# One reciprocal for the forward scans' first values, and a reordered start, in a gated-linear-attention and SoLU kernel

## The chip, the cores and the metric

The kernel runs on one core of one Trainium2 chip, as one launch. The metric is the device time of that launch in microseconds (us); "before" is the kernel without the change. In the profile PE is TensorE's matmuls, PEld its weight loads, DVE is VectorE, ACT ScalarE, POOL GpSimd and SP SyncE, which only issues DMAs. L12 is line 12 of the kernel before.

## The reference, cut to what matters

```python
# q, k, v, alpha: (4, 8, 768, 48); alpha lies between 0.8 and 1.0
for t in range(768):
    state = alpha[:, :, t, :, None] * state + k_t (outer) v_t      # per batch and head
    y[:, :, t] = q_t @ state
x = y as (3072 tokens, 384)
h = x @ w_in                                    # 384 -> 1024
solu = h * softmax(h)
ln = (solu - mean) / sqrt(var + 1e-6) * g_ln
out = ln @ w_out                                # 1024 -> 384
```

All is float32, except that the three weights arrive as float64.

## The kernel before, in words

**Tiling.** The 768 tokens are cut into G = 6 groups of 128. A group holds those 128 tokens of all four batches, thus 512 columns. Inside a group the recurrence is done in one piece: with the products of alpha along the tokens, the scores of the group's tokens are a masked matrix, and what came before enters through a state per head, updated once a group.

**Layout of the attention.** Alpha, k and q are turned so that channels lie on partitions and tokens along the row: 12 rows of 129 values (`aT`, `hT`, `kT`, `qv` and `qe`), in three parts of four rows (NP = 4). Parts 0 and 1 hold the first 32 channels of the eight heads, part 2 the last 16 of all heads. In group 0 TensorE turns them (`turned`, L158, against the identity `ident`), with the last 16 channels copied together first by ScalarE (`ends_of`, L151); later groups use VectorE's transposes (`firsts`, `lasts`, `alpha_T`).

**The scans.** `scan_back` (L206) forms with a VectorE scan the product of alpha from the end of the group backwards; its first column (`h4[:, :, 1]`) is the decay over the whole group, and the keys are multiplied by it. `scan_on` (L211) forms the same products forwards, as a scan that starts from the reciprocal of that column, with `seed` as its second operand: all zero except for the first value of each row. For each part it limits the column from below to 1e-13 (`least`, L218), takes the reciprocal into one of two seed tiles (L219) and scans in place in `aT` (L220, recorded as L204). In its call for part 2 it also copies the column to `fend` (L215), which a check at the end of the kernel compares with 1e-13 (L949). The queries are multiplied by the result. Where any of the checks fails, a general path runs after this one.

**The start (group 0, L643 to L760).** SyncE's queue loads alpha, k, q, v and the first raw weights, in this order, from L643 on; ScalarE's queue loads the identity, the mask, `parity` and the gains (L644 to L648). VectorE sets `ones`, `mone` (minus one, a bias of the alpha check) and others; GpSimd zeroes `vn`, `unit`, `seed`, `state` and `kg`. `warm(18)` (L673, products in L446) multiplies ones by ones on TensorE until alpha is there. Then alpha is turned into three PSUM tiles, ScalarE copies them (L677) and VectorE scans back; k is turned; then scan on for part 2, the keys' products (L685), scan on for part 0, the queries' products for parts 2 and 0 (L693), scan on for part 1 and its product. ScalarE's `apart` (L246) splits part 2 of the queries by parity. `scores` (L274) multiplies queries and keys, first half (heads 0 to 3), then second half; `masked` (L288) multiplies by the mask on VectorE; `read_values` (L352) multiplies the values by the masked scores. After that VectorE turns the float64 weights into float32 in eight pieces (`bits`, L584), between the steps of the first group's up-projection (`up_mm`, `up_act`), and ScalarE checks their range (`in_range`, L574).

**Order.** Every engine runs its instructions in the order written in the code. Group 1's attention is written out at L744 to L800, between the down-projections of group 0 (`down`, `finish`); group 2's scans, keys and first forward scans at L801 to L811. Then a hand-written plan (`usual` and `first`, L815 to L826) places the steps of the next group's attention among the eight up-projections of the present group; "on2 on0 on1" are the three forward scans, which for groups 3 to 5 come with the second up-projection.

**Around the change.** `finish` (L506) takes four small VectorE steps (L519 to L528), GpSimd's power (L532) and ScalarE's scaling, then issues the output. `up_act` (L396) frees the PSUM tile of an up-projection with L405. `decay` (L258) multiplies the state by the group's decay on GpSimd, which `ends_of_decay` (L242) and the DMAs of `move_lasts` and `move_firsts` (L230 to L240) bring into place, and `read_state` (L344) multiplies the queries by it. `keys` (L226) multiplies keys by the backward products on GpSimd, and `queries` (L253) the queries by the forward ones. `alpha_over` (L192) checks on ScalarE that alpha lies within -1 and 1. `far` keeps sums of the weights' check.

Of the kernel before, what the change touches and what calls it, by code (L numbers as in the profile page):

```python
# [9 lines left out]
FP = mybir.dt.float32  # L10
# [3 lines left out]
AF = mybir.ActivationFunctionType  # L14
ALU = mybir.AluOpType
AX = mybir.AxisListType
P = 128
# [15 lines left out]
def fast_path(ctx, tc, q, k, v, alpha, moe_w_in, moe_w_out, moe_g_ln, out):  # L33
# [12 lines left out]
    nc = tc.nc  # L46
# [5 lines left out]
    NP = H // 2  # L52
    NB = H + NP
# [5 lines left out]
    LEAST = 1e-13  # L59
# [5 lines left out]
    const = pool("const", 1)  # L65
    ring = pool("ring", 3)
    work = pool("work", 2)
    small = pool("small", 4)
# [4 lines left out]
    ps_a = pool("ps_a", 1, space=PS)  # L73
# [13 lines left out]
    mone = const.tile([P, 1], FP, name="mone")  # L87
# [8 lines left out]
    fend = const.tile([P, G, NB], FP, name="fend")  # L96
# [12 lines left out]
    SW = P + 1  # L109
# [1 line left out]
    lots = [lot[:, 768 * i : 768 * i + 768] for i in range(4)]  # L111
    q64 = lot[:, 0 : 2 * H * SW].rearrange("p (c h t) -> p c h t", c=2, h=H)
    aT = const.tile([P, NB, SW], FP, name="aT")
    seed = [const.tile([P, NP, SW], FP, name=f"seed{i}") for i in range(2)]
    unit = const.tile([P, NP, SW], FP, name="unit")
    hT = const.tile([P, NB * SW + 2], FP, name="hT")
    h4 = hT[:, 0 : NB * SW].rearrange("p (j s) -> p j s", s=SW)
# [25 lines left out]
    def load_first(src, dst, g):  # L143
        t = slice(g * P, (g + 1) * P)
        for b in range(0, B, 2):
            nc.sync.dma_start(
                out=by_token(dst)[:, b : b + 2].rearrange("p b h d -> p (b h) d"),
                in_=src[b : b + 2, :, t].rearrange("b h p d -> p (b h) d"),
            )
# [42 lines left out]
    def alpha_over(g):  # L192
        x = an.rearrange("p h u d -> p (h u d)")
        sq = one.tile([P, 768], FP, name="sq").bitcast(U8)[:, 0 : x.shape[1]]
        for i, sign in enumerate((1.0, -1.0)):
            nc.scalar.activation(  # L196
                out=sq, in_=x, func=AF.Relu, scale=sign, bias=mone, accum_out=over[:, g, i : i + 1]
            )

    def scan(out, data, start, flip):  # L200
        a, o, s = (x.rearrange("p j s -> p (j s)") for x in (data, out, start))
        if flip:
            a, o, s = a[:, ::-1], o[:, ::-1], s[:, ::-1]
        nc.vector.tensor_tensor_scan(out=o, data0=a, data1=s, initial=1.0, op0=ALU.mult, op1=ALU.add)  # L204

    def scan_back(g, i):  # L206

        part = slice(NP * i, NP * i + NP)
        scan(h4[:, part], aT[:, part], unit, True)

    def scan_on(g, i):  # L211
        part = slice(NP * i, NP * i + NP)
        s = seed[i % 2]
        if i == 2:
            nc.vector.tensor_copy(out=fend[:, g], in_=h4[:, :, 1])  # L215

        least = small.tile([P, NP, 1], FP, name="least")
        nc.vector.tensor_scalar(out=least, in0=h4[:, part, 1:2], scalar1=LEAST, scalar2=None, op0=ALU.max)  # L218
        nc.vector.reciprocal(out=s[:, :, 0:1], in_=least)  # L219
        scan(aT[:, part], aT[:, part], s, False)  # L220

    def keys_T(g):
        firsts(kn, kT[:, 0:H])
        lasts(kn, kT[:, H:NB])
# [21 lines left out]
    def apart():  # L246
        for i in range(2):
            nc.scalar.mul(
                out=qv[:, H : 2 * H, 0:P].rearrange("p (j i) t -> p j i t", i=2)[:, :, i], in_=qe[:, :, 0:P],
                mul=parity[:, i : i + 1],  # L250
            )
# [22 lines left out]
    def scores(g, half, a=None):  # L274
        a = a or banks("a", [NP, P])
        for i in range(NP):
            h = half * NP + i
            for kb, qb in ((h, h), (H + h // 2, H + h)):
                for b in range(B):
                    nc.tensor.matmul(  # L280
                        a[b][:, i], lhsT=kT[quarter(b), kb], rhs=qv[quarter(b), qb, 0:P], start=kb == h, stop=kb != h,
                        tile_position=(32 * b, 0), skip_group_check=True,
                    )
        masks[half] = a
# [158 lines left out]
    def warm(n, ps=ps_o, tag="o"):  # L443
        t = ps.tile([P, 512], FP, tag=tag, name="warm")
        for i in range(n):
            nc.tensor.matmul(t[:, 0:P], lhsT=ones, rhs=ones, start=True, stop=True)  # L446
# [124 lines left out]
    far = const.tile([P, len(pieces), 2], FP, name="far")  # L571
# [47 lines left out]
    def mean(half):  # L619


        m = ps_h.tile([P, 512], FP, tag="h", name="sums")[:, 0:DM]
        if half == 0:
            for f in range(FC):
                r = quarter(f % 4)
                nc.tensor.matmul(
                    m[r], lhsT=ones[:, 0:32], rhs=w_out[:, f, 0:DM], start=f < 4, stop=f >= FC - 4,
                    tile_position=(0, r.start), skip_group_check=True,
                )
            made["m"] = work.tile([P, DM], FP, name="o_mean")  # L630
            nc.scalar.mul(out=made["m"], in_=m, mul=-1.0 / (32 * DFF))
        else:
            nc.tensor.matmul(m, lhsT=ones, rhs=made["m"], start=True, stop=True)
            nc.scalar.copy(out=mean_sb, in_=m)
# [5 lines left out]
    def inline(x, name):  # L640
        return nc.inline_tensor(np.ascontiguousarray(x, np.float32), name=name).ap()

    load_first(alpha, an, 0)  # L643
    nc.scalar.dma_start(out=ident, in_=inline(np.eye(P), "ident_c"))  # L644
    nc.scalar.dma_start(out=mask, in_=inline(np.triu(np.ones((P, P))), "mask_c"))
    odd = np.arange(P) // E1 % 2
# [6 lines left out]
    nc.gpsimd.memset(unit[:, :, 0:1], 1.0)  # L653
    nc.gpsimd.memset(aT[:, :, 0:1], 0.0)
    nc.gpsimd.memset(hT[:, NB * SW : NB * SW + 2], 1.0)
    for s in seed:
        nc.gpsimd.memset(s, 0.0)
    nc.gpsimd.memset(state, 0.0)
    nc.gpsimd.memset(kg, 0.0)
    load_v(0)  # L660
# [2 lines left out]
    nc.vector.memset(ones, 1.0)  # L663
    nc.vector.memset(small_ones, 1.0 / 32)
    nc.vector.memset(mhalf, -0.5)
    nc.vector.memset(mone, -1.0)
    nc.vector.memset(w_out[:, :, DM : DM + 1], 1.0)

    def three(name, where):
        return [pool.tile([P, NP, P], FP, tag=tag, name=f"{name}{i}") for i, (pool, tag) in enumerate(where)]  # L670


    warm(18)  # L673
    t = three("tp_a", [(ps_a, "a0"), (ps_a, "a1"), (ps_a, "a2")])
    turned(an, ends_of(an, 1), t)
    for i in range(3):
# [2 lines left out]
    t = three("tp_k", [(ps_a, "a3"), (ps_h, "h"), (ps_h, "h")])  # L679
    turned(kn, ends_of(kn, 2), t)  # L680
    alpha_over(0)
    scan_on(0, 2)
    for i in range(3):
        part = slice(NP * i, NP * i + NP)
# [4 lines left out]
    for i in (2, 0, 1):  # L689
        if i == 1:  # L690
            scan_on(0, i)
        part = slice(NP * i, NP * i + NP)
        nc.vector.tensor_tensor(  # L693
            out=qe[:, :, 0:P] if i == 2 else qv[:, part, 0:P], in0=t[i], in1=aT[:, part, 1:SW], op=ALU.mult
        )
        if i == 2:
            apart()
    scores(0, 0)
    t = [x.tile([P, NP, P], FP, tag=n, name="a_" + n) for x, n in ((ps_h, "h"), (ps_o, "o")) for _ in range(2)]
    scores(0, 1, t)  # L700
# [58 lines left out]
    for i in range(3):  # L759
        scan_back(1, i)  # L760
        part = slice(NP * i, NP * i + NP)
        nc.vector.tensor_tensor(out=kT[:, part], in0=tk[i], in1=hk[:, part], op=ALU.mult)
    mean(0)
    down(0, 1)
    mean(1)
# [14 lines left out]
    for i in range(2):  # L780
        scan_on(1, i)
        part = slice(NP * i, NP * i + NP)
# [19 lines left out]
    load(alpha, an, 3)  # L802
    for i in range(3):
        scan_back(2, i)
    keys_T(2)
    keys(2)
    load(k, kn, 3)
# [20 lines left out]
    def attend(a, what):  # L828

        more = a + 1 < G  # L830
        if what == "v":
            load_v(a)
        elif what == "keys":
            keys_T(a)
            keys(a)
            if more:
                load(k, kn, a + 1)
        elif what[:2] == "on":
            scan_on(a, int(what[2]))
        elif what == "lasts":  # L840
            lasts(qn, qe[:, :, 0:P])
            ends_of_decay()
            queries(2)
            move_lasts()
        elif what == "firsts":
            firsts(qn, qv[:, 0:H, 0:P])
            queries(0)
            queries(1)
            move_firsts()
            if more:  # L850
                load(q, qn, a + 1)
        elif what == "apart":
            apart()
        elif what == "decay":
            decay(a)
        elif what == "keys_back":
            if more:
                keys_back(a)
        elif what[:6] == "scores":
            scores(a, int(what[6]))  # L860
        elif what[:6] == "masked":
            masked(int(what[6]))
        elif what == "alpha" and more:
            alpha_T(a + 1)
            if a > 2:
                attend(a, "over")
        elif what == "over" and more:
            alpha_over(a + 1)
            if a + 2 < G:
                load(alpha, an, a + 2)  # L870
        elif what == "back" and more:
            for i in range(3):
                scan_back(a + 1, i)
        elif what == "begin":
            read_begin()
        elif what[:4] == "read":
            read_state(int(what[4]))
        elif what == "values":
            read_values(a)
        elif what == "kv" and more:  # L880
            next_state(a)
# [533 lines left out]
```

## Time and profile before

| What | Value |
|---|---|
| Time, median of 3 runs (lowest to highest) | 382.9 us (382.52 to 383.46) |
| The profiled execution's own time, and its span | 382.77 us, 381.0 us |
| TensorE's matmuls, busy | 363.3 us |
| VectorE, busy | 251.2 us |
| ScalarE, busy | 144.3 us |
| GpSimd, busy | 112.1 us |
| L218 `least`, 18 times: shortest, median, longest | 136, 157, 733 ns |
| L219 reciprocal, 18 times | 179, 180, 182 ns |
| L215 `fend`, 6 times | 158, 271, 626 ns |
| L204 forward scan, 18 times | 1232, 1232, 1968 ns |
| L446 warming products, 36 records, first to last start | 1.0 to 7.2 us |

The profile is that of one execution; its times are counted from the first instruction. A row of the order of time gives start and length, engine, line, operation, what it writes and reads, the sizes, how many such instructions in a row were merged, and in brackets how long the engine had stood idle before it and what ended that. An engine name with a q is its queue, which waits or issues DMAs. A float32 matmul leaves two records. A list of waits gives, for an engine and line, who ended its idle time, the total in us, how often, and the longest.

### The profile page before, as it was taken

Reading aid. Unit: us, or ns where it says so; the run is one execution under the profiler, and the core shown is the slowest. Engines: PE = TensorE matmul, PEld = TensorE weight load, DVE = VectorE, ACT = ScalarE, POOL = GpSimd, SP = SyncE. Lnnn points to the kernel's source line nnn. Section 1 sums busy time; section 2 is a strip of 40 time slices with the busy share of each in tenths; the row PEclk is TensorE's granted clock in tenths of the full one; section 3 lists DMA queues with packets and bytes.
Section 4 is the critical chain, followed back from the end, with each engine's and each line's share of the span. In section 5 each row is a group of like instructions: output and inputs, shape, how many; then the busy total and the mean of one; then the engine's idle time right before and its main releaser. Section 6 shows DMA issues by size and latency. Waiting matters only on the chain. (4 is left out here: it accounts for less than half of the span.)

```text
span 381.0 us, 10060 instructions
## 1 busy us (share of the span) xinstructions
PE 363.3 (95%) x4341; PEld 215.7 (57%) x4341; DVE 251.2 (66%) x413; ACT 144.3 (38%) x255; POOL 112.1 (29%) x122
## 2 busy tenths in 40 slices
PE   8789899988999999999999999999999999999994
PEld 8675335656654656555665555665556565555552
DVE  0999878996999779884665875666874414444500
ACT  2628566681155436143261153341241132322100
POOL 6000000000243990455210465111475211332200
PEclk9999999999999999999999999999999999999999
DMA  9982978248239611927041627004023000000011
GB/s 181 179 322 88 204 208 207 44 95 184 66 88 190 149 44 46 199 64 181 2 105 47 142 69 168 21 5 96 10 77 78 22 2 21 23 22 21 22 45 48
DMA packets 72438, 36.05 MB, mean 95 GB/s; under 512 B 48184, under 2 KB 69952, under 8 KB 72384
## 3 DMA queue, kind: packets, MB, share of 16 engines
q1 hardware_dynamic: 71360, 34.39, 38.3%
q10 hardware_dynamic: 1024, 0.92, 0.7%
q8 instruction: 36, 0.59, 0.7%
q14 instruction: 18, 0.15, 0.1%
HBM read 25.30 MB, written 4.72 MB: 79 GB/s over the span
## 5 line engine op out<-in xcount | busy, mean ns | idle before, releaser
L390 PE MATMUL h<-x,w_in 128*128 128x512 f32 x288 | 133.4, 601 | 3.9 <-DVE room L405 2.7
L501 PE MATMUL o<-w_out,room 128*128 128x385 f32 x384 | 133.6, 492 | 1.1 <-DVE least L218 1.1
L501 PEld LDWEIGHTS o<-w_out,room 128*128 128x128 f32 x384 | 71.1, 189 | 56.0 <-issue 14.9
L390 PEld LDWEIGHTS h<-x,w_in 128*128 128x128 f32 x288 | 52.4, 189 | 63.3 <-issue 47.5
L405 DVE TENSOR_TENSOR room<-h,e 128x512 f32<-128x512 f32 x40 | 27.7, 693 | 58.1 <-ACT e L404 58.1
L404 ACT ACTIVATE e<-h 128x512 f32<-128x512 f32 x40 | 23.9, 597 | 88.9 <-PE h L390 88.7
L421 POOL TENSOR_TENSOR p<-p,e 128x512 f32<-128x512 f32 x30 | 40.8, 1361 | 26.5 <-ACT e L404 26.0
L406 ACT ACTIVATE u<-room 128x512 f32<-128x512 f32 x40 | 25.2, 630 | 44.0 <-DVE room L405 44.0
L532 POOL TENSOR_TENSOR r<-sums,mhalf 128x1 f32<-128x1 f32 x20 | 12.5, 626 | 86.9 <-DVE sums L524 86.8
L291 DVE TENSOR_TENSOR sT<-a,mask 128x512 f32<-128x512 f32 x44 | 27.3, 682 | 14.2 <-PE a L280 14.2
L421 DVE TENSOR_TENSOR p<-p,u 128x512 f32<-128x512 f32 x30 | 24.3, 810 | 8.4 <-ACT u L406 8.4
L280 PE MATMUL a<-qv,kT 32*128 32x128 f32 x704 | 24.9, 278 | 3.9 <-DVE least L218 1.8
L280 PEld LDWEIGHTS a<-qv,kT 32*128 32x128 f32 x704 | 22.0, 186 | 10.9 <-POOL p L421 2.2
L204 DVE TENSOR_TENSOR_SCAN hT<-aT,unit 128x516 f32<-128x516 f32 x18 | 22.2, 1278 | 8.3 <-ACT aT L677 8.3
L204 DVE TENSOR_TENSOR_SCAN aT<-aT,seed 128x516 f32<-128x516 f32 x18 | 24.4, 1355 | 0.6
L329 PE MATMUL y<-sT,vn 128*32 128x128 f32 x768 | 22.9, 274 | 0.8 <-issue 0.5
L329 PEld LDWEIGHTS y<-sT,vn 128*32 128x32 f32 x768 | 20.8, 110 | 4.2 <-issue 3.4
L228 POOL TENSOR_TENSOR kT<-kT,hT 128x1024 f32<-128x1024 f32 (+1 forms) x8 | 13.3, 1683 | 28.7 <-DVE kT L179 28.7
L196 ACT ACTIVATE sq<-an,mone 128x1536 uint8<-128x1536 f32 x12 | 18.9, 1574 | 0.2
L534 ACT ACTIVATE o_sb<-o,r 128x384 f32<-128x384 f32 x16 | 9.3, 581 | 25.1 <-POOL r L532 25.1
L243 POOL COPY qe<-hT 128x4 f32<-128x4 f32 x5 | 1.0, 191 | 58.5 <-DVE hT L204 58.5
L359 ACT COPY x<-y 128x384 f32<-128x384 f32 x24 | 11.2, 479 | 14.6 <-PE y L329 14.4
(142 smaller groups left out, 367.7 us busy)
## 6 DMA issues: line engine op xcount, KB each, us to landing
vn<-in_v_dram SPq DMA_DIRECT2D x24, 192.0 KB, 4.6
an<-in_alpha_dram SPq DMA_DIRECT2D x20, 192.0 KB, 4.5
out_dram<-o_sb SPq DMA_DIRECT2D x20, 192.0 KB, 1.9
room<-in_moe_w_in_dram SPq DMA_DIRECT2D x6, 512.0 KB, 7.7
room<-in_moe_w_out_dram SPq DMA_DIRECT2D x8, 384.0 KB, 4.4
kn<-in_k_dram SPq DMA_DIRECT2D x16, 192.0 KB, 4.4
qn<-in_q_dram SPq DMA_DIRECT2D x16, 192.0 KB, 4.4
lot<-qe SPq DMA_DIRECT2D x40, 64.5 KB, 2.1
```

The source lines that it names most:

```text
L196: nc.scalar.activation(out=sq, in_=x, func=AF.Relu, scale=sign, bias=mone, accum_out=over[:, g, i : i + 1])
L204: nc.vector.tensor_tensor_scan(out=o, data0=a, data1=s, initial=1.0, op0=ALU.mult, op1=ALU.add)
L228: nc.gpsimd.tensor_tensor(out=kT[:, part], in0=kT[:, part], in1=hk[:, part], op=ALU.mult)
L280: nc.tensor.matmul(a[b][:, i], lhsT=kT[quarter(b), kb], rhs=qv[quarter(b), qb, 0:P], start=kb == h, stop=kb != h, tile_position=(32 * b, 0 ...
L291: nc.vector.tensor_tensor(out=sT[:, b, half * NP : half * NP + NP], in0=a[b], in1=mask[:, None, :].to_broadcast([P, NP, P]), op=ALU.mult,)
L329: nc.tensor.matmul(y_bank(b)[quarter(r), a], lhsT=lhsT, rhs=rhs, start=(b, r) not in begun, stop=stop, tile_position=(row, 32 * r), skip_g ...
L390: nc.tensor.matmul(h, lhsT=w_in[:, a, f * P : (f + 1) * P], rhs=d["x"][:, a].rearrange("p b t -> p (b t)"), start=(a == 0), stop=(a == KC ...
L404: nc.scalar.activation(out=e, in_=h, func=AF.Exp)
L405: nc.vector.tensor_tensor(out=u, in0=h, in1=e, op=ALU.mult)
L406: nc.scalar.activation(out=u2, in_=u, func=AF.Square)
L421: eng.tensor_tensor(out=p, in0=d[0][i] if f == 1 else p, in1=d[f][i], op=ALU.add)
L501: nc.tensor.matmul(d["o"][:, 0 : DM + 1], lhsT=u_of(g, f)[:, b * P : b * P + P], rhs=w_out[:, f], start=(f == 0), stop=(f == FC - 1), skip ...
```

## The change

- `scan_on` no longer copies `fend`, limits the column or takes reciprocals. A new `inverses(g)` copies the column to `fend` on GpSimd and takes one reciprocal of all 12 values straight from the column into one `seed` tile of 12 rows. It is called once a group: ahead of the first forward scan of group 0; after the backward scans and key products of group 1; between the backward scans and `keys_T` of group 2; ahead of "on2" for groups 3 to 5.
- The limit of 1e-13 is gone from the reciprocal; the check of `fend` against it stays.
- `mone` is set as VectorE's first instruction, and ScalarE takes an Exp of it (into a cell of `far` that is written again later) ahead of the four constant loads in its queue.
- `warm(14)` stands in place of `warm(18)`, and `warm(2)` comes ahead of the first scores of group 0, into the PSUM tile that those scores use for batch 1.

```diff
-    seed = [const.tile([P, NP, SW], FP, name=f"seed{i}") for i in range(2)]
+    seed = const.tile([P, NB, SW], FP, name="seed")
...
+    def inverses(g):
+        nc.gpsimd.tensor_copy(out=fend[:, g], in_=h4[:, :, 1])
+        nc.vector.reciprocal(out=seed[:, :, 0:1], in_=h4[:, :, 1:2])
+
     def scan_on(g, i):
         part = slice(NP * i, NP * i + NP)
-        s = seed[i % 2]
-        if i == 2:
-            nc.vector.tensor_copy(out=fend[:, g], in_=h4[:, :, 1])
-
-        least = small.tile([P, NP, 1], FP, name="least")
-        nc.vector.tensor_scalar(out=least, in0=h4[:, part, 1:2], scalar1=LEAST, scalar2=None, op0=ALU.max)
-        nc.vector.reciprocal(out=s[:, :, 0:1], in_=least)
-        scan(aT[:, part], aT[:, part], s, False)
+        scan(aT[:, part], aT[:, part], seed[:, part], False)
...
     load_first(alpha, an, 0)
+    nc.vector.memset(mone, -1.0)
+    nc.scalar.activation(out=far[:, 0, 1:2], in_=mone, func=AF.Exp)
     nc.scalar.dma_start(out=ident, in_=inline(np.eye(P), "ident_c"))
...
-    for s in seed:
-        nc.gpsimd.memset(s, 0.0)
+    nc.gpsimd.memset(seed, 0.0)
...
-    nc.vector.memset(mone, -1.0)
...
-    warm(18)
+    warm(14)
...
     alpha_over(0)
+    inverses(0)
     scan_on(0, 2)
...
+    warm(2, ps_a, "a1")
     scores(0, 0)
...
+    inverses(1)
     mean(0)
...
         scan_back(2, i)
+    inverses(2)
     keys_T(2)
...
         elif what[:2] == "on":
+            if what == "on2":
+                inverses(a)
             scan_on(a, int(what[2]))
```

## The prediction

> **What bounds the kernel now.** I read the busy shares first, then who TensorE waits for, then the order of time in the stretches where it waits.
>
> ```profile
> PE 363.3 (95%) x4341; PEld 215.7 (57%) x4341; DVE 251.2 (66%) x413; ACT 144.3 (38%) x255; POOL 112.1 (29%) x122
> ```
>
> TensorE (PE) is busy for 95% of the span, so all but 17.7 us is its own work. The change removes no matmul that counts, only warming products. It can win only where TensorE waits. The longest waits of PE:
>
> ```profile
> engine line waited for: us in total, times, longest us
> PE h L390 <- DVE room L405: 2.7, 4, 0.9
> PE a L280 <- DVE least L218: 1.8, 1, 1.8
> PE a L280 <- DVE qv L783: 1.2, 1, 1.2
> PE o L501 <- DVE least L218: 1.1, 1, 1.1
> ...
> PE tp_q L164 <- DMA qn<-in_q_dram: 1.0, 2, 0.9
> ...
> PE a L280 <- ACT qv L248: 0.3, 1, 0.3
> PE a L280 <- POOL qv L256: 0.3, 1, 0.3
> ```
>
> By the table of stretches, PE idles in the start (0 to 31 us), at 41, 45, 55 and 77, at 82 to 88 (group 1), at 114 to 125 (group 2), at 145, and in the tail. From 150 to 360 it never idles, so whatever is won before 145 reaches the end unchanged, and VectorE (DVE) work saved after that is worth nothing. The start, in order of time:
>
> ```profile
> 6.83 1.28 ACT L155 ACT_TABLE_LOAD   x1 [6.83 <-DMA an<-in_alpha_dram]
> 7.37 1.96 PE L164 MATMUL tp_a<-ident,an 128*32 128x128 f32 x64
> ...
> 9.33 3.48 DVE L204 TENSOR_TENSOR_SCAN hT<-aT,unit 128x516 f32<-128x516 f32 x3 [8.26 <-ACT aT L677]
> ...
> 14.72 1.83 PE L164 MATMUL tp_q<-ident,qn 128*32 128x128 f32 x58 [0.86 <-DMA qn<-in_q_dram]
> ...
> 17.90 0.67 DVE L693 TENSOR_TENSOR qe<-tp_q,aT 128x512 f32<-128x512 f32 x1
> ...
> 21.43 2.47 DVE L291 TENSOR_TENSOR sT<-a,mask 128x512 f32<-128x512 f32 x4
> ```
>
> VectorE looks like the chain, since it hardly rests between 9.33 and 36. But at 17.90 it is only 0.3 us behind something else: q lands at 14.7, and its transposes run on PE until 17.5. That is the key to the start.
>
> **What the Trainium skill says.** "ScalarE: Activation LUTs", What ACT_TABLE_LOAD costs, gives about 1283 ns for a load; the row shows 1.28 us, and the trace has one load in all, so a first Exp moves it and adds none. "TensorE: Matmul & The Clock Gate", Part 1, says the array runs at half clock until it has been busy for some 3.4 us and falls back only after an idle window of that order; the records of the warming products agree in kind (0.213 us start to start up to 5.3 us, 0.111 after). "DMA: Bandwidth & Descriptors", Issuing engines are not separate DMA queues, says transfers of ScalarE's and SyncE's queues share the same engines; the DMA row is at 9 from 2 to 13 us, so delaying the constants brings q no sooner. "SBUF — State Buffer", on the shared port pair, says VectorE operations with two SBUF inputs block while GpSimd holds the pair; L521 and L524 below agree.
>
> **The change part by part.** Times are those of the profiled execution (382.77 us, span 381.0, 1.8 around it), 0.1 below the median of 382.9.
>
> *Warming and tables.* 14 products end at about 6.4 instead of 7.4 (8 fewer records of 0.111 us). Alpha's second half lands at 6.75 (ScalarE's wait shows it: 6.83), so the transposes start at 6.85 instead of 7.37: 0.52 sooner. ScalarE's table load, moved to about 1 us, lets its first copy start at 6.85 instead of 8.12. The first aT copy then waits for PE alone, and the scans start at 8.8 instead of 9.33: **0.53 sooner**. The price is that four constant loads queue behind the Exp on ScalarE: the identity issues at about 2.4 instead of 0.74. Before, it landed 2.0 us after issue, the mask 3.3 us after its own under traffic; so 4.4 to 5.7, before alpha. Mask, parity and gains are needed at 21, 18 and 28.
>
> *One reciprocal.* Before the first forward scan the copy, maximum and reciprocal take 12.85 to 13.41, 0.56 us. One reciprocal of 12 values remains; the trace shows only 4 values (0.18) and copies of 12 at 0.17, so between 0.18 and 0.28 with its wait. I take 0.25: **0.3 saved**. The scans of parts 0 and 1 lose 16.34 to 16.75 and 19.08 to 19.56: **0.4 each**. GpSimd's copy (0.19, as L243) delays only its own queue: ends_of_decay in group 1, product sums later, both with slack; GpSimd idles for 58 us before the first of these. The larger seed memset ends GpSimd's start at 7.4 instead of 6.9, unneeded before 12.
>
> *What the start is worth.* The DVE could reach qe at 16.7 (17.90 - 0.53 - 0.3 - 0.4). It can't use it: q's transposes end at 17.54, so qe starts at 17.60: 0.30 sooner. The scores start at 19.0. The scan of part 1 is 0.8 sooner, but the mask waits for the first scores, which take 2.1 us: 21.13 instead of 21.43. The weights' bits, next on DVE, then start at 25.9; their third transfer landed at 25.3, so it doesn't bind. **0.30 won**; everything to 76 us hangs on this and shifts along. Two products ahead of the scores run in PE's idle time from 17.5 to 19.3 (4 records of 0.11): nothing. If q lands x sooner, the start wins 0.30 + x, at most 0.85, where those weights bind; at least 0 if q is 0.3 late.
>
> *Group 1.* The scans lose 0.26, 0.42 and 0.41 (80.09 to 80.58, 83.50 to 83.92, 85.79 to 86.20). PE's waits of 1.1 and 1.2 shrink, and it would be 1.1 sooner at 88.21. But then:
>
> ```profile
> 97.78 1.42 PE L329 MATMUL y<-lot,state 64*32 64x128 f32 x64
> ```
>
> ```profile
> 96.34 1.78 POOL L264 TENSOR_TENSOR state<-state,lot 128x384 f32<-128x384 f32 x2 [7.10 <-DMA lot<-qv]
> ```
>
> The reading of the state needs GpSimd's decay, done at 97.2 and 98.13, and already PE stops inside that row, at 97.96 to 98.18. The decay hangs on SyncE's queue: alpha's load released by the alpha check (80.67), q's, then the moves of q, back to back to 95.3, landing at 97.2. No part of the change touches that, so PE arrives 1.1 sooner and waits. **0 won** here beyond the start's 0.3.
>
> *Group 2.*
>
> ```profile
> 108.00 1.35 DVE L521 SCALAR_TENSOR_TENSOR t<-sums 128x1 f32<-128x1 f32 x1
> 109.39 1.11 DVE L524 TENSOR_TENSOR sums<-t,s 128x1 f32<-128x1 f32 x1
> ...
> 114.12 0.66 DVE L405 TENSOR_TENSOR room<-h,e 128x512 f32<-128x512 f32 x1
> ```
>
> L521 and L524 usually take 0.16; here they end with GpSimd's key products (107.16 to 110.48). The reciprocal moves ahead of the keys: +0.2 there, perhaps +0.1 left. From 110.94 to 111.42 (0.48) and 112.57 to 112.97 (0.4) the DVE loses 0.88, so L405 ends 0.78 sooner at least, and PE's wait of 0.80 at 114.83 goes: **0.80**. Then scan part 1 loses 116.57 to 117.55 (0.98, for its maximum also met GpSimd). The chain lasts, firsts, GpSimd's query products, ScalarE's apart is some 1.5 sooner, and PE's waits of 0.31 and 0.32 (124.4, 125.4) shrink; PE comes 0.8 sooner itself, so I keep **0.5** of 0.63. ScalarE's wait at 145 (0.6) stays.
>
> Sum: 0.30 + 0 + 0.80 + 0.50 = 1.60 on 382.77: **381.2**. Groups 3 to 5 and the tail: nothing, PE is full.
>
> **The rivals.** *More of it counts* (0.18): q lands sooner, or the DVE reaching the decay's neighbourhood sooner frees GpSimd. For: the start has 1.2 us of unused savings. Against: the DMA row is full, SyncE's queue is fixed. Start 0.85 and 0.3 more later: 380.4. *Less of it counts* (0.24): DVE's small operations of group 2 land on GpSimd's decay and keys again, or q lands 0.3 later. For: L521 and L524 wait wherever GpSimd works. Only 0.3 to 0.8 is left: 382.2. *Slower* (0.08): fewer warming products leave PE idle from 6.4 to 6.85 and its clock falls back. Then 96 records of alpha and as many of k at 0.05 instead of 0.027 cost 2.2 us each, of which k's is half hidden by DMA: some 3.3 more, less 1.6: 384.5. It decides only if an idle of half a microsecond is enough; against it, after 1.8 us of idle at 17.5 the scores ran at full rate (64 records in 2.08 us). That the change does nothing at all is not possible, as each removed row is on DVE.
>
> **How the numbers follow.** The forecast has 0.50, with a range of its own of 380.7 to 381.7. A measurement here tells about 0.3% from no change, so faster is below 381.75: most of the forecast (0.46) and the first rival (0.18), 0.64. Within 0.3%: the rest of the forecast and the second rival, 0.28. Slower 0.08. The range reaches from the middle of the first rival, 380.2, to most of the second, 382.4; outside lie the last rival and the ends of the others.
>
> **What would show it.** The first scan near 8.8; a DVE wait of about 0.9 for q's transposes, near 17.6, then one for the scores near 21; in group 1 no waits of PE on DVE at 83 and 88 but a new one of about 1 us on GpSimd's decay near 97; no wait for L405 near 114. I am wrong if q's landing moves, if the decay comes sooner, or if the identity lands after alpha.

## The result, and the profile after

The changed kernel takes 380.75 us (median of 5 runs, 380.43 to 381.39) where the kernel before took 382.63 (382.2 to 383.46) in the same comparison: a ratio of 0.9939, 95% interval 0.992 to 0.9958. The medians differ by 1.9 us, and the interval stands for 1.6 to 3.1; the profiled executions differ by 2.02 (382.77 to 380.75; spans 381.0 to 378.9). The forecast was 1.6 less. To read the ratios below one has to know that in the three later comparisons 31 of 98 runs of the kernel before, and 4 of 71 of the kernels with the new reciprocals, had a mean granted clock under 0.997 and mostly took 1.3 us or more longer than the rest; without them ("at full clock" below) the medians of before are 382.43, 382.50 and 382.36, the change is worth 1.5 us (e5) to 1.7, and what a ratio shows beyond that is that such runs are rarer. Line numbers below are those of the changed kernel (L405 of before is L402, L404 L401, L406 L403, L501 L498, L280 L277, L329 L326, L264 L261, L519 L516, L521 L518, L524 L521); for before, e1 and e8 they are the old ones.

The busy line of the page after the change:

```profile
PE 362.4 (96%) x4337; PEld 215.1 (57%) x4337; DVE 246.0 (65%) x377; ACT 144.7 (38%) x256; POOL 120.5 (32%) x127
```

VectorE has 36 instructions and 5.2 us less; GpSimd has 8.4 us more. TensorE's waits, as the list for PE gives them:

```profile
PE h L387 <- DVE room L402: 2.1, 4, 0.9
PE tp_q L164 <- DMA qn<-in_q_dram: 1.4, 1, 1.4
...
PE o L498 <- DVE o_mean L525: 0.9, 1, 0.9
PE a L277 <- DVE qv L691: 0.8, 1, 0.8
...
PE a L277 <- DVE sums L516: 0.4, 1, 0.4
PE a L277 <- ACT qv L245: 0.3, 1, 0.3
PE y L326 <- POOL state L261: 0.3, 1, 0.3
PE y L326 <- issue: 0.2, 1, 0.2
```

The waits of 1.8 and 1.1 that `least` ended and that of 1.2 for `qv` have not gone; they are shorter, and other instructions of VectorE end them: 0.8 (`qv`), 0.9 (`o_mean`) and 0.4 (`sums`). Most of what the first lost is the two warming products ahead of the scores, which now fill 0.71 of it. Of L402's, 0.6 went. The 0.3 for GpSimd's decay is new. The start of the changed kernel, in order of time:

```profile
0.74 1.28 ACT L642 ACT_TABLE_LOAD   x1 [0.74 <-PEq L1402]
...
0.91 0.35 ACTq L643 DMA_DIRECT2D ident<-ident_c  x1
...
8.80 3.48 DVE L204 TENSOR_TENSOR_SCAN hT<-aT,unit 128x516 f32<-128x516 f32 x3 [7.70 <-ACT aT L674]
...
12.39 0.23 DVE L213 RECIPROCAL seed<-hT 128x12 f32<-128x12 f32 x1
...
14.80 1.83 PE L164 MATMUL tp_q<-ident,qn 128*32 128x128 f32 x58 [1.41 <-DMA qn<-in_q_dram]
...
17.67 0.69 DVE L691 TENSOR_TENSOR qe<-tp_q,aT 128x512 f32<-128x512 f32 x1 [0.86 <-PE tp_q L164]
...
21.20 2.48 DVE L288 TENSOR_TENSOR sT<-a,mask 128x512 f32<-128x512 f32 x4 [0.38 <-PE a L277]
```

The scans begin at 8.80, the 12-value reciprocal takes 0.23, and then VectorE stands idle for 0.86 until q's transposes are through: q landed no sooner (14.8, before 14.7). The first up-projection starts at 30.66 (before 30.88), the second at 40.97 (before 41.37).

Group 2, in order of time:

```profile
106.18 3.33 POOL L225 TENSOR_TENSOR kT<-kT,hT 128x1024 f32<-128x1024 f32 x2 [2.15 <-DVE kT L179]
...
107.09 1.29 DVE L518 SCALAR_TENSOR_TENSOR t<-sums 128x1 f32<-128x1 f32 x1
...
108.42 1.10 DVE L521 TENSOR_TENSOR sums<-t,s 128x1 f32<-128x1 f32 x1
...
109.97 2.34 DVE L204 TENSOR_TENSOR_SCAN aT<-aT,seed 128x516 f32<-128x516 f32 x2
...
112.24 0.66 DVE L402 TENSOR_TENSOR room<-h,e 128x512 f32<-128x512 f32 x1
...
112.95 2.84 PE L387 MATMUL h<-x,w_in 128*128 128x512 f32 x6 [0.31 <-DVE room L402]
```

The two forward scans stand together, and L402 starts 1.88 us sooner than before (114.12). L518 and L521 still end with GpSimd's key products (109.51).

To see where the time went I cut the span at three places. The first is the start of the second up-projection on PE. The other two are on VectorE: the turning of group 2's alpha (L179, its first transposes after group 1), and the first L402 of group 2. A further point inside group 1 is L516 (L519 of before), the first of the small steps that `finish` takes just ahead of that turning. Each column is the gain against the profile of before, in us.

| Kernel | start, to 41.4 | group 1, to 98.8 | of it, to L516 | group 2, to 114.1 | rest | whole span |
|---|---|---|---|---|---|---|
| before, its own length | 41.37 | 57.41 | 56.10 | 15.34 | 266.9 | 381.0 |
| the prediction | 0.30 | 0 |  | 0.80 | 0.50 | 1.6 |
| changed | 0.40 | 0.89 | 1.10 | 0.59 | 0.2 | 2.1 |
| e5, the changed kernel again | 0.33 | 0.60 | 1.07 | 0.57 | 0.5 | 2.0 |
| e1, start only | 0.40 | 0.07 | 0.04 | -0.07 | 0.0 | 0.4 |
| e2, reciprocals only | -0.13 | 1.41 | 1.11 | 0.55 | 0.2 | 2.0 |
| e6, old warming | 0.02 | 0.71 | 1.12 | 0.51 | 0.5 | 1.7 |
| e7, copy on VectorE | 0.27 | 0.93 | 0.99 | 0.50 | 0.4 | 2.1 |
| e3, q later | 0.51 | 1.47 | 1.14 | 0.58 | 0.4 | 3.0 |
| e9, q later, copy on VectorE | 0.33 | 1.37 | 1.04 | 0.57 | 0.4 | 2.7 |
| e10, q and mask later | -0.46 | 1.38 | 1.05 | 0.58 | 0.4 | 1.9 |
| e8, before with q later | 0.36 | 0.32 | -0.01 | -0.03 | 0.1 | 0.7 |

### The profile page after: what moved, and what is told of

Same layout as the page of the kernel before. It is cut to its first block, busy times and chain, and to the rows that moved or that the text cites. A ratio compares the mean times of both kernels' runs of the same rounds, so it can differ in the third digit from the quotient of the medians.

```text
span 378.9 us, 10022 instructions
## 1 busy us (share of the span) xinstructions
PE 362.4 (96%) x4337; PEld 215.1 (57%) x4337; DVE 246.0 (65%) x377; ACT 144.7 (38%) x256; POOL 120.5 (32%) x127
## 3 DMA queue, kind: packets, MB, share of 16 engines
HBM read 25.30 MB, written 4.72 MB: 79 GB/s over the span
## 5 line engine op out<-in xcount | busy, mean ns | idle before, releaser
L498 PE MATMUL o<-w_out,room 128*128 128x385 f32 x384 | 133.6, 492 | 0.9 <-DVE o_mean L525 0.9
L498 PEld LDWEIGHTS o<-w_out,room 128*128 128x128 f32 x384 | 71.1, 189 | 55.7 <-issue 13.8
L402 DVE TENSOR_TENSOR room<-h,e 128x512 f32<-128x512 f32 x40 | 27.6, 690 | 61.1 <-ACT e L401 61.1
L401 ACT ACTIVATE e<-h 128x512 f32<-128x512 f32 x40 | 23.8, 596 | 96.0 <-PE h L387 95.8
L403 ACT ACTIVATE u<-room 128x512 f32<-128x512 f32 x40 | 25.2, 630 | 36.4 <-DVE room L402 36.4
L288 DVE TENSOR_TENSOR sT<-a,mask 128x512 f32<-128x512 f32 x44 | 27.3, 683 | 14.8 <-PE a L277 14.8
L277 PEld LDWEIGHTS a<-qv,kT 32*128 32x128 f32 x704 | 21.9, 186 | 8.7 <-POOL p L418 1.6
L277 PE MATMUL a<-qv,kT 32*128 32x128 f32 x704 | 24.8, 278 | 1.8 <-DVE qv L691 0.8
L212 POOL COPY fend<-hT 128x12 f32<-128x12 f32 x6 | 4.1, 680 | 69.9 <-DVE hT L204 69.9
L204 DVE TENSOR_TENSOR_SCAN aT<-aT,seed 128x516 f32<-128x516 f32 x18 | 25.4, 1442 | 0.2
L326 PE MATMUL y<-sT,vn 128*32 128x128 f32 x768 | 22.9, 274 | 1.0 <-DVE sT L288 0.8
L326 PEld LDWEIGHTS y<-sT,vn 128*32 128x32 f32 x768 | 20.9, 110 | 4.3 <-issue 3.1
```

What stands on the lines that cost most here:

```text
L277: nc.tensor.matmul(a[b][:, i], lhsT=kT[quarter(b), kb], rhs=qv[quarter(b), qb, 0:P], start=kb == h, stop=kb != h, tile_position=(32 * b, 0 ...
L288: nc.vector.tensor_tensor(out=sT[:, b, half * NP : half * NP + NP], in0=a[b], in1=mask[:, None, :].to_broadcast([P, NP, P]), op=ALU.mult,)
L326: nc.tensor.matmul(y_bank(b)[quarter(r), a], lhsT=lhsT, rhs=rhs, start=(b, r) not in begun, stop=stop, tile_position=(row, 32 * r), skip_g ...
L401: nc.scalar.activation(out=e, in_=h, func=AF.Exp)
L402: nc.vector.tensor_tensor(out=u, in0=h, in1=e, op=ALU.mult)
L403: nc.scalar.activation(out=u2, in_=u, func=AF.Square)
```

## The experiments

The theory after the result (Q in the texts on record): in the start only q's landing counts; in group 1 PE's gain ends at GpSimd's decay, which SyncE's queue sets; in group 2 VectorE's savings count. Its rival is that the start is an ordinary chain of VectorE, in which every saved piece counts.

**e1: the new start alone.** The kernel before, with

```diff
+    nc.vector.memset(mone, -1.0)
+    nc.scalar.activation(out=far[:, 0, 1:2], in_=mone, func=AF.Exp)
...
-    nc.vector.memset(mone, -1.0)
...
-    warm(18)
+    warm(14)
...
+    warm(2, ps_a, "a1")
```

> The kernel before with the changed start alone (Exp ahead of the constant loads, 14 warming products, 2 ahead of the scores); the old copies, limits and reciprocals stay. Theory Q (the start hangs on q's transfer): the scans back begin near 8.8 instead of 9.33, yet the first query product begins near 17.6 and the first up-projection is only 0.2 to 0.3 us sooner; nothing is won in groups 1 and 2, so the kernel is 0.2 to 0.6 us faster. Rival V (the start hangs on VectorE's own work): 0.53 at the scans reaches the up-projection whole, 0.5 us or more.

Measured: 382.33 us (22 runs) beside 382.74, ratio 0.9988 (0.9976 to 1.0); at full clock the gain is 0.1. The scans begin at 8.64, and the first up-projection at 30.68. Between them VectorE waits for q:

```profile
17.68 0.69 DVE L694 TENSOR_TENSOR qe<-tp_q,aT 128x512 f32<-128x512 f32 x1 [0.39 <-PE tp_q L164]
```

So the start reaches its limit, q, without the reciprocals, and the 1.1 us that these save there buy nothing more. In group 2 PE gains nothing by it: the wait for L405 grew from 0.80 to 1.15.

**e2: the reciprocals alone.** The changed kernel with all the edits of e1 taken back.

> The changed kernel with the old start (no Exp ahead, 18 warming products, none ahead of the scores). Theory Q: VectorE gets to the first query product 0.5 us later than in the changed kernel, but still before q's transposes end, so the start wins the same 0.2 to 0.3 us and the whole is within 0.3 us of the changed kernel: 1.5 to 2.0 us faster than before. Rival V: 0.5 us of the gain goes missing, 1.3 to 1.5 us faster.

Measured: 381.11 (22 runs), ratio 0.9959 (0.9945 to 0.9972), so 1.6 us by the medians and 1.4 at full clock, which can't tell Q from V. `qe` starts at 17.65, as with both. This is the profile that corrects my theory. Its order of time around the decay, on GpSimd and PE, then on VectorE, and last the two rows of before that go with it:

```profile
97.28 0.84 POOL L261 TENSOR_TENSOR state<-state,lot 128x384 f32<-128x384 f32 x1 [0.43 <-DMA lot<-qv]
...
98.18 1.01 PE L326 MATMUL y<-lot,state 64*32 64x128 f32 x48 [0.72 <-POOL state L261]
```

```profile
97.50 2.06 DVE L179 STREAM_TRANSPOSE aT<-an 128x1024 f32<-128x1024 f32 x1
...
112.29 0.66 DVE L402 TENSOR_TENSOR room<-h,e 128x512 f32<-128x512 f32 x1
```

```profile
98.18 0.75 PEld L329 LDWEIGHTS y<-lot,state 64*32 64x32 f32 x48 [0.22 <-POOL state L264]
...
98.78 2.03 DVE L179 STREAM_TRANSPOSE aT<-an 128x1024 f32<-128x1024 f32 x1
```

PE resumes at 98.18, to the hundredth where it did before: it gets past the decay no sooner, as predicted. But VectorE doesn't stop there. It turns group 2's alpha at 97.50 (before 98.78), and L402 begins at 112.29, as good as in the changed kernel (112.24), whose decay ended 1.1 us sooner. VectorE carries the 1.3 us past PE's wait, and PE collects it in group 2: it gains 1.25 by L402 and 2.00 by 125, where 1.30 were predicted.

**e3: the queries of group 2 loaded later.** If SyncE's queue sets the decay, then taking a load from in front of its moves should free it. The changed kernel with

```diff
     tq += three("tp_q2", [(ps_h, "h")])
     turned(qn, ends_q, tq, range(H, NB))
-    load(q, qn, 2)
...
     move_firsts()
+    load(q, qn, 2)
```

> The changed kernel with group 2's load of q issued behind the moves of group 1's queries instead of ahead of them. Theory D (the reading of the state in group 1 waits for GpSimd's decay, which waits for SyncE's queue): the decay ends some 2 us sooner, near 95, TensorE's wait for it near 97 goes, and the reading comes 0.3 to 0.4 us sooner; 0.2 to 0.4 us faster than the changed kernel if group 2 passes it on. Rival: TensorE is late for other reasons there and nothing moves, or q's later landing holds group 2's queries near 117 and it is slower.

Measured: 380.12 (6 runs, 379.79 to 380.61), ratio 0.9924 (0.9903 to 0.9945); that is 0.6 to 0.9 below the changed kernel's medians in this document (380.75 and 381.01), more than the 0.2 to 0.4 expected. SyncE's queue in this kernel (start, length), then GpSimd, PE and VectorE:

```profile
82.00 5.25 SPq L232 DMA_DIRECT2D lot<-qe  x8
...
91.24 2.28 SPq L134 DMA_DIRECT2D qn<-in_q_dram  x4
```

```profile
92.60 1.65 POOL L261 TENSOR_TENSOR state<-state,lot 128x384 f32<-128x384 f32 x2 [5.01 <-DMA lot<-qv]
...
96.12 1.17 PE L326 MATMUL y<-lot,state 64*32 64x128 f32 x64
```

```profile
96.00 0.16 DVE L518 SCALAR_TENSOR_TENSOR t<-sums 128x1 f32<-128x1 f32 x1
96.19 0.16 DVE L521 TENSOR_TENSOR sums<-t,s 128x1 f32<-128x1 f32 x1
...
96.80 2.04 DVE L179 STREAM_TRANSPOSE aT<-an 128x1024 f32<-128x1024 f32 x1
```

The decay is done at 94.24 (changed kernel 97.02) and PE doesn't wait for it. There is a second gain that I had not expected: the decay no longer lies beside VectorE's small steps of `finish`. L518 and L521 take 0.16 each; in the changed kernel the pair took 0.16 and 0.69, in e5 0.34 and 0.77. So VectorE wins 1.47 in group 1, where it wins 0.89 in the changed kernel and 0.60 in e5; up to L516 all three are alike (1.14, 1.10, 1.07).

**e4: less before q.** The changed kernel with half of group 0's k left out of the load:

```diff
-    load_first(k, kn, 0)
+    nc.sync.dma_start(
+        out=by_token(kn)[:, 0:2].rearrange("p b h d -> p (b h) d"),
+        in_=k[0:2, :, 0:P].rearrange("b h p d -> p (b h) d"),
+    )
+    nc.gpsimd.memset(by_token(kn)[:, 2:4], 0.05)
```

> The changed kernel without the load of the second half of group 0's keys (two batches get a constant instead of k; that part of the reference is not computed). It takes 0.4 MB out of the queue ahead of q. Theory Q: q lands about 1.8 us sooner, near 13, the first query product begins near 16.7 where VectorE's own work then bounds it, and the first up-projection is 0.8 to 1.0 us sooner than in the changed kernel. Rival V: q's landing moves and the query product does not.

Measured, in a single run: 381.63. q landed at 12.99, `qe` started at 16.56 and the mask's first product at 20.06, 1.14 sooner than in the changed kernel: q it is. But the first up-projection came 0.47 later than there (31.12). The table of stretches (PE, PEld, DVE, ACT and POOL busy with counts, then granted clock, DMA share and GB/s) of this kernel, and then of the changed one:

```profile
20.00:25.40 5.40, 3.55 (x111) 3.00 (x107) 5.34 (x9) 0.00 (x0) 0.00 (x0) 1.00 0.86 322
25.40:28.80 3.40, 3.40 (x75) 3.40 (x69) 3.26 (x5) 1.13 (x3) 0.00 (x0) 0.51 0.04 11
```

```profile
25.20:28.60 3.40, 3.30 (x102) 3.08 (x102) 3.30 (x6) 1.68 (x4) 0.00 (x0) 1.00 0.57 230
```

TensorE had stood idle for 0.81 us before 23.2 and for 1.04 before 24.98, and then its clock was halved for one stretch of 3.4 us, in which it issued 75 records where the changed kernel issues 102. So this run shows that q's landing moves `qe` and the mask, but not that the up-projection would follow. It is the price that my "slower" rival names, at another place. Idle times like these don't cost the clock every time: e10 has 0.81 and 1.17 nearly as close together and keeps it (the last section has the difference).

**e5: the changed kernel again**, with no edit, beside e6 and e7.

> The changed kernel once more, as the measure for the three runs beside it. In its first profile GpSimd's decay of group 1 came 1.1 us sooner than before, though the start had won only 0.4. Theory T (that 0.7 is the luck of transfers, not the change): in a second profile the decay ends between 0.3 and 1.1 sooner than before, at another time than 97.0. Rival: it ends at 97.0 again within 0.1. Time 1.7 to 2.1 us faster than before.

Measured: 381.01 (8 runs), ratio 0.994 (0.9922 to 0.9958). The decay ended at 97.39, not 97.02, and PE waited for it twice, 0.45 in all. So its early end in the first profile was no property of the kernel, and neither is the time at which PE gets past it.

**e6: the old warming.** The changed kernel with

```diff
-    warm(14)
+    warm(18)
...
-    warm(2, ps_a, "a1")
```

> The changed kernel with the old warming (18 products, none ahead of the scores); the Exp and the reciprocal stay. Theory I (TensorE ran out of instructions near 25 us, and their fetch comes 0.4 us later with the old warming, since in two profiles with it the gap ended at 25.7 and with the new one at 25.1 to 25.3): the gap ends near 25.7 again and the wait for L402 near 41 ends about 0.5 us later than in the changed kernel; 0.3 to 0.5 us slower than it. Rival C (the warming serves the clock alone): the gap ends near 25.3 as in the changed kernel, and only single runs, with a lower granted clock, are 1 us or more slower. Rival N: no difference at all.

Measured: 381.19 (17 runs), ratio 0.9952 (0.9938 to 0.9966), which can't be told from e5. In the profile the second up-projection starts at 41.35, 0.38 later than in the changed kernel (0.31 later than in e5), where TensorE's stall in front of L326 (under e10 below) ended at 25.63 and not at 25.30. The runs don't show the 0.3 to 0.5 expected, and e10, with the new warming, has the longest stall of all.

**e7: the column's copy back on VectorE.**

```diff
-        nc.gpsimd.tensor_copy(out=fend[:, g], in_=h4[:, :, 1])
+        nc.vector.tensor_copy(out=fend[:, g], in_=h4[:, :, 1])
```

> The changed kernel with the check's copy put back on VectorE. My sum took the move to GpSimd as worth about 0.1 us (hidden behind q in the start and behind the decay in group 1, 0.1 in group 2): 0.0 to 0.2 us slower than the changed kernel. Rival: GpSimd's copy costs more than it saves where GpSimd and VectorE share a port, and this is faster.

Measured: 380.65 (6 runs), ratio 0.9929 (0.9906 to 0.9952), against 381.01 for e5. With 6 and 8 runs that 0.36 is no firm difference, but moving that copy to GpSimd wins nothing that can be measured. On VectorE it moves the reciprocal by 0.09 us; on GpSimd six such copies take 4.1 us, 0.68 each.

**e8: the later load in the kernel before.** The edit of e3, without the change.

> The kernel before with group 2's load of q behind the moves of group 1's queries, nothing else. Theory D: there TensorE reaches the reading of the state only at 97.8, so an early decay wins no more than the stop inside that row: 0.2 to 0.4 us faster than before, against 0.6 in the changed kernel; the savings of group 1 count only together with an early decay. Rival: the later load is worth the same in both, 0.6 or more.

Measured: 383.09 (20 runs), ratio 1.0001 (0.9986 to 1.0016). The interval is too wide for the 0.2 to 0.4 expected, and the runs at full clock (382.50 both) show nothing. In the profile group 1 gains 0.32: its L521, 0.49 before, takes 0.16. PE waits 1.0 for L405 afterwards. So the early decay alone is worth 0.3 at most. It is worth more with the change because the small steps have more to lose there: from L516 to the turning of alpha it is 1.31 us in before, 1.52 in the changed kernel and 1.78 in e5, and 0.98 in both e3 and e8.

**e9: e3 with the copy on VectorE**, thus the edits of e3 and e7.

> The changed kernel with the load of group 2's queries moved behind the moves of group 1 (380.12 us in an earlier comparison), and with the copy of the decay's column back on VectorE. If that copy counts only through GpSimd's queue, it is worth nothing here too: 380.1, within 0.3. If the copies by GpSimd hold back its decay and products where an early decay has just made GpSimd the later engine in groups 1 and 2, moving them back wins 0.3 to 0.6: 379.6.

Measured: 380.19 (6 runs, 379.92 to 381.06), beside 382.36 for before in this comparison, ratio 0.9945 (0.9931 to 0.9959). Nothing, as in e7.

**e10: the mask behind q.** e3 with

```diff
-    nc.scalar.dma_start(out=mask, in_=inline(np.triu(np.ones((P, P))), "mask_c"))
...
     turned(qn, ends_of(qn, 3), t)
+    nc.scalar.dma_start(out=mask, in_=inline(np.triu(np.ones((P, P))), "mask_c"))
```

> The changed kernel with the load of group 2's queries moved as before, and the mask's load (64 KB) put in ScalarE's queue behind the copy of q's last channels, so after q has landed. If q's landing is set by the bytes that all queues move before it (the start's DMA row is full), 64 KB at 180 to 320 GB/s bring it 0.2 to 0.35 us sooner: q lands near 14.45 instead of 14.8, qe and the mask's first product come 0.2 to 0.35 sooner, 379.8. If SyncE's own issuing and its queue set the landing, as the prediction took it, q lands at 14.8 still and nothing is won: 380.1. If the mask lands after 21.2 in the traffic of the values, the start loses what it is late.

Measured: 380.12 (6 runs, 379.87 to 380.99), ratio 0.9941 (0.9927 to 0.9956). q landed at 14.61 (e3 14.82, e9 14.84), the mask's first product began at 21.05 (e3 21.26), and the first up-projection at 30.57 (30.72). In the profiles of this document that load all of k and the mask, q lands between 14.68 and 14.84, so this one is 0.07 to 0.23 sooner. The prediction had it that delaying the constants would bring q no sooner; this speaks against it, but one profile doesn't settle a tenth of a microsecond. The median doesn't move either, and this profiled execution, at 380.99, is one of two among the six that lie 1.0 above the other four. Its order of time on PE, then on ScalarE:

```profile
26.09 3.03 PE L326 MATMUL y<-sT,vn 128*32 128x128 f32 x99 [1.17 <-issue]
...
41.83 0.70 PE L387 MATMUL h<-x,w_in 128*128 128x512 f32 x1 [1.66 <-DVE room L402]
```

```profile
26.54 0.48 ACT L356 COPY x<-y 128x384 f32<-128x384 f32 x1 [6.96 <-PE y L326]
...
41.81 0.63 ACT L403 ACTIVATE sT<-room 128x512 f32<-128x512 f32 x1 [3.15 <-DVE room L402]
```

TensorE stood for 1.17 us in front of L326 with nothing to wait for ("issue"). ScalarE's copies of x, its range checks, L401 and L403 follow it one by one, so the second up-projection is 0.86 later than in the changed kernel, though the first was sooner.

That stall is listed in ten of the twelve profiles, with 0.20 to 1.17 us (before 0.48, ending at 25.67; changed 0.23, at 25.30; e2 0.82, at 25.77), and not in e3 and e8. It lies at one place among PE's instructions: 13 records after the wait for `sT` in the kernels with the old warming, and 17 in those with the new, which has four records fewer ahead of it. In all ten it ends 1.25 to 1.50 us after the end of a 16 KB packet of the DMA queue whose kind is "instruction". In e3 and e8 PE goes on from the same place at 25.09 and 25.23, 1.32 and 1.25 after that packet, but it had reached the place so late that no stall shows. So PE seems to wait there for its next instructions; this is argued from the traces, for no run moves the packet. In e8, the start of before without the stall, the second up-projection starts at 41.01; in e3, the new start without it, at 40.86.

## Why the prediction was right, and where not

**The start: right in mechanism and size, with a second end that I didn't see.** The scans came at 8.80 as predicted, the wait for q's transposes was 0.86 (about 0.9), `qe` came at 17.67 (17.60), the wait for the scores was there (0.38), and the first up-projection gained 0.22 of 0.30, since q landed 0.08 later. "Everything to 76 us hangs on this and shifts along" was wrong: from 25 us on a second chain, PE's reading of values, ScalarE's copies and checks, ends later, at the second up-projection. There the profile shows 0.40, of which the stall before L326 is a part. Between the two profiles without a stall (e3 and e8) the start is worth 0.15, and e1 at full clock 0.1; it was half as much as I took, or less. The identity was issued at 0.91, not 2.4: ScalarE's queue went on issuing DMAs while the table loaded (0.74 to 2.02). It landed at 3.88, well ahead of alpha, and TensorE's clock didn't fall here.

**Group 1: the step that failed.** "PE arrives 1.1 sooner and waits. 0 won here" is right for PE and wrong for the kernel. PE did arrive 1.1 sooner (88.21 became 86.70, of which the start is 0.4), and did wait on the decay: 0.3 in the changed kernel, 0.45 in e5, 0.72 in e2. What PE itself gained in group 1 followed the luck of the decay's transfers: 0.7, 0.4 and 0.1. But the wait stops PE alone. VectorE's next work, `finish` and group 2's alpha, hangs on what PE did before the wait, so VectorE keeps its lead: 0.60 to 1.41 us in the five profiles with the reciprocals and SyncE's old order. Rows of before, and then of the changed kernel:

```profile
97.47 0.15 DVE L519 COPY sums<-o 128x1 f32<-128x1 f32 x1
97.66 0.49 DVE L521 SCALAR_TENSOR_TENSOR t<-sums 128x1 f32<-128x1 f32 x1
```

```profile
95.32 1.70 POOL L261 TENSOR_TENSOR state<-state,lot 128x384 f32<-128x384 f32 x2 [7.59 <-DMA lot<-qv]
95.97 0.15 DVE L516 COPY sums<-o 128x1 f32<-128x1 f32 x1
...
96.35 0.69 DVE L521 TENSOR_TENSOR sums<-t,s 128x1 f32<-128x1 f32 x1
...
97.49 2.05 DVE L179 STREAM_TRANSPOSE aT<-an 128x1024 f32<-128x1024 f32 x1
```

The table's column to L516 parts the lead from what becomes of it. Up to there the eight profiles with the reciprocals win 0.99 to 1.14, and the two without (e1, e8) 0.04 and -0.01; the steps that I took out of group 1 come to 0.26 + 0.42 + 0.41 = 1.09. So the lead is there whole in each, and the rest of the spread is how the decay falls beside L518 and L521: from L516 to the turning of alpha it is 1.31 in before, 1.01 in e2, 1.78 in e5, and 0.98 where the decay is over by then (e3, e8, e9, e10). "SBUF — State Buffer" of the Trainium skill, SBUF: two separate sides, says of the shared port pair that the one who comes second blocks fully; the trace agrees, for L521 of the changed kernel, begun inside the decay's second product, ends at 97.04, 0.02 after it. Two of the prediction's signs failed with this step: PE's waits on VectorE at 83 and 88 stayed, with 0.9 and 0.4, and the one for the decay was 0.3 to 0.7, not about 1. And the decay did come sooner, by 1.1 in the first profile and 0.7 in e5, which I had named as a sign of being wrong.

**Group 2: the mechanism right, the term too large by 0.2.** L402 gains 0.50 to 0.59 in this stretch where 0.80 were predicted. The removed steps were worth what was worked out: from the end of GpSimd's keys to L402 it is 2.73 where it was 3.64 (109.51 to 112.24, 110.48 to 114.12), 0.91 less. But I had let L518 and L521 swallow all but 0.1 of the reciprocal put ahead of the keys. It costs 0.30 (from the backward scans to the keys' transposes 3.63, before 3.33), and since GpSimd's keys start later by it and those two steps end with the keys, nothing is swallowed. The wait for L402 went only from 0.80 to 0.31, because PE, too, was sooner there. In e2, e6 and e7, where the decay holds PE longer, it is gone. The later 0.50 became 0.2 to 0.5: POOL's wait of 0.31 is gone, ScalarE's of 0.32 stays at 123.04. The copies of `ends_of_decay`, 0.19 before, took 1.14 and 0.71 beside the scan of part 1.

**The copy to GpSimd** was costed at nothing on GpSimd's side and at 0.1 to 0.2 saved on VectorE; e7 and e9 show no gain at all.

**The sum.** 0.30 + 0 + 0.80 + 0.50 = 1.60 stands against 0.40 + 0.89 + 0.59 + 0.2 = 2.1 in the profile, and 1.5 to 1.7 at full clock. That the total is this close is in part luck: I wrote off 0.9 in group 1, and overrated the start, group 2 and what follows, each by 0.1 to 0.3. "Slower" did not occur in the changed kernel's profiles: from 5.6 us to the last few microseconds the clock is full. "More of it counts" was nearest in size but not in cause, for q didn't land sooner and GpSimd's decay is not what was won.

**A better version.** With q's load moved (e3, e9, e10) the medians are 380.12, 380.19 and 380.12, 0.5 to 0.9 below those of the changed kernel (380.75 and 381.01), but never measured side by side with it. Their ratios to before (0.9924, 0.9945, 0.9941) have intervals that overlap with the change's own 0.9939, so how much better is not settled. The table has 1.4 for group 1 in all three, against 0.89 and 0.60 for the change as it is (but e2 has 1.41 without the move, after a later start).

**Left open:** why the 16 KB packet before PE's stall begins at 22.6 in one execution and at 23.5 in another. No run was made that moves it.

## What to carry to other kernels

When an engine's wait swallows a saving, ask which engine stops there: the one that made the saving may run on, keep its lead and hand it over at the next place where it is waited for. Cut the span at points on the engine that was relieved, not only on the busiest one. And look at what a late transfer is queued behind: a load moved behind the moves that are waited for frees both the waiting engine and the small steps beside which the late work falls.

## What the runs showed of the hardware

- **A stall after an instruction packet.** TensorE stood for 0.2 to 1.2 us without any semaphore and went on 1.25 to 1.50 us after a 16 KB packet of the "instruction" kind had ended, at a fixed place among its records. The second up-projection came at 40.86 in e3, which shows no stall, and at 41.83 in e10, which has the longest.
- **Half clock for one stretch.** In e4 the clock was halved from 25.48 for 3.41 us, after idle times of 0.81 and 1.04 us within 2.6 us (22.4 to 24.98). "TensorE: Matmul & The Clock Gate", Part 1, gives that length for a window, and the trace agrees; but PE was by no means idle for all of the window before. I cut the twelve profiles into stretches of 3.41 us in step with the clock's records and summed PE's idle time in each (estimates, since the ends of matmuls are modelled). The stretch before the drop had 1.85 us. Once the clock was full, stretches with up to 1.67 were all followed by full clock and those with 2.1 and more by half, while one with 1.94 (e10, at the end) kept it. e10's idle times of 0.81 and 1.17 fell into two stretches. The kernel before has 1.77 us of idle PE in the 3.41 from 17.5, and the changed kernel nowhere more than 1.41 between 5 and 140. That may be why a lower clock is rarer with the change, but this is not shown: no trace of before has such a stretch at half clock.
- **Reused semaphores hold a queue.** In the kernel before each of the last four moves of `qe` issued just as one of q's four loads landed (87.90, 88.61, 89.61 and 90.37, landings at 87.88, 88.60, 89.59 and 90.36), and they take those loads' semaphores. With q's load behind the moves all eight issued between 82.00 and 86.65.
- **A small copy beside a scan.** GpSimd's copies of 4 and 8 values per partition took 0.19 and 0.20 alone and 1.14 and 0.71 beside VectorE's scan.
